# Second half of batch 0's heads by casting loads, and the opening of an attention and gated feed-forward kernel in another order

## The chip, the cores and the metric

The kernel runs on one core of one Trainium2 chip. The metric is the device time of one execution in microseconds (us); smaller is better. The kernel before was timed in five runs: 320.38 us in the median, from 320.23 to 320.91. A profile was taken of one further execution; its own time stands in the table below.

## What is computed

Eight batches of linear attention, whose normed result is the input of a gated feed-forward block with a residual:

```python
kv  = einsum('bhsd,bhse->bhde', k, v)          # b=8, h=8 heads, s=576 tokens, d=e=64
out = einsum('bhsd,bhde->bhse', q, kv)
x   = out / sqrt(mean(out*out, -1) + 1e-6) * g_norm      # reshaped to 4608 x 512
ffn = (gelu(x @ w_gate) * (x @ w_val)) @ w_out           # w_gate, w_val: 512 x 1536; w_out: 1536 x 512
y   = x + sigmoid(x @ w_res) * ffn
```

All inputs are float32 in memory; the kernel multiplies in float16 and accumulates in float32.

## The kernel before

**Blocks.** Of each batch's 576 tokens the first 512 make one block (4 tokens on each of 128 partitions); the last 64 of every batch are gathered in a ninth block at the end. The attention of the next batches is worked out beside the feed-forward of the present one, at places written out by hand. Every engine runs its instructions in the order in which the program records them; the schedule is manual. The engines are TensorE (PE in the profile), VectorE (DVE), ScalarE (ACT) and GpSimd (POOL). SyncE (SP) and POOL issue most of the transfers.

**The opening.** Batch 0 has nothing in front of it that could hide its attention, so it is done in pairs of heads (pr 0 to 3), in an order written out as a string of words, `opening` (L1294 to L1299). The words are run one by one by `f_piece` (L1243); a word is a name, the pair and, where it can be chosen, the engine (A = ACT, D = DVE, P = POOL). The words that the texts below use:

- `qc`, `kc`, `vc` (f_cast, L1134 and L1132): cast a pair of heads of q, k, v from float32 to float16.
- `qT` (L1158), `qo` (L1161): transpose q of a pair on PE into a PSUM bank, and copy it out.
- `kv` (L1169, L1175), `kvo` (L1178): the product of k and v of a pair, 4 matmuls for the 512 tokens and 2 for the last 64 (which `lk`, L1143, and `lv`, L1152, prepare), and its copy under a mask that keeps the two heads apart.
- `o` (L1184), `sq` (L1192), `rd` (L1195), `rt` (L1201), `ri` (L1205), `t` (L1209): q times kv, squares on ACT, their sums on DVE, root on ACT, reciprocal and scaling on DVE.
- `xT` (L1219), `xo` (L1226, L1224): transpose the result and copy it out times the norm's weight.
- `g`, `v` (L1235): the pair's part of the first two columns of `x @ w_gate` and `x @ w_val`, with weight columns 0 to 255 (`wg0`, `wv0`).
- `warm` (L1111): matmuls on zeros whose result is not used.
- `wg`, `wv` (L148): issue a load of weight columns on POOL; `wcg`, `wcv` (L1264): cast weight columns.

**Where the data come from.** A load issued on SP moves float32 as it is; one issued on POOL casts to float16 on its way. All of batch 0 comes through SP (L1039, L1055, L1077): heads 0 to 3 of q, of k, k's and v's last tokens, v; then pairs 2 and 3 of each; then weight columns 0 to 255 of both matrices. Casting is done by the engines: per pair one instruction each for q, k and v, and four for the weights. For batch 0 the casts of q and k also reorder from by-head to by-token (`[P, NJ, H, D]`), so that one pair's 128 columns of k are the stationary operand of one matmul. In later batches POOL's loads cast, k stays by head, and `kv_mm` (L208) uses 64 columns per matmul, one head each, in two halves of the PSUM partitions.

**What follows the opening.** From L410 on, PE runs the feed-forward of block 0 for weight columns 2 to 11, then L946, L430, L447 and the next block. POOL issues the loads of the other weights and of batch 1 (L148, L1600, L120 to L122, L109, L157); at most eight loads of POOL are under way, and the ninth waits for the first. PSUM has eight banks of 2 KB per partition: four taken in turn for the attention (`pattn`), four for the feed-forward (`pmoe`).

```python
    opening = """
    qc1P qc0A qT1 qT0 kc1P kc0A qo0D warm3 lk0D lv0P qo1A warm3 vc1D vc0A kv1 qc2A kv0 kvo1 kvo0 o1 kc2P qT2
    lk1P sq1 qo2D o0 warm3 warm2 vc2P sq0 lv1A rd1 kv2 qc3P rt1 kvo2 rd0 kc3A qT3 wg1 wv1 ri1 o2 rt0 t1 warm3 warm1 sq2 vc3D
    rd2 qo3A xT1 kv3 wg2 wcg0P rt2 kvo3 ri0 ri2 warm2 o3 t2 xo1A wcg1P sq3a wcv0P sq3b g1 xT2 rd3a wcv1P rd3b
    wv2 t0 rt3 xo2A wg3 wv3 v1 xT0 ri3 xo0A g2 v2 t3a t3b xT3a xT3b g0 xo3aA xo3bD gelu v0 g3a v3a g3b v3b
    """
```

Of the kernel before, what the change touches and what calls it, by code (L numbers as in the profile page):

```python
# [8 lines left out]
FP32 = mybir.dt.float32  # L9
FP16 = mybir.dt.float16  # L10
# [8 lines left out]
def kernel(  # L19
# [27 lines left out]
    WCS = (256, 256, 512, 512)  # L47
# [24 lines left out]
                self.turn.append(bank)  # L72
            return psum.tile(shape, dtype, tag=f"bank{bank}", name=name)

    pmoe, pattn = Banks(3, 1, 0, 2, opening=(0, 1, 2)), Banks(4, 5, 6, 7)

    def banks_behind():

# [14 lines left out]
    def rows4(t, b, lo, hi):  # L93
        return t[b, lo:hi, 0:M0, :].rearrange("h (p j) d -> p h (j d)", j=NJ)
# [55 lines left out]
    def load_wg(i):  # L150
        load_columns(wg_c, moe_w_gate, i)
# [38 lines left out]
    def halves(e):  # L190
        return slice(e * D, (e + 1) * D)
# [846 lines left out]
    def load_first(which, t, lo, hi):  # L1038
        nc.sync.dma_start(out=raw[0, which][:, lo:hi, :], in_=rows4(t, 0, lo, hi))  # L1039
# [22 lines left out]
    for which, t in (("q", q), ("k", k), ("v", v)):  # L1062
        load_first(which, t, 0, HH)
        if which == "k":
            load_first_last(0)
    for pr in range(NP // 2, NP):
        load_first("q", q, 2 * pr, 2 * pr + 2)
        load_first("k", k, 2 * pr, 2 * pr + 2)
        if pr == NP // 2:
            load_first_last(1)  # L1070
        load_first("v", v, 2 * pr, 2 * pr + 2)
    w_raw = {}
    for n, t in (("g", moe_w_gate), ("v", moe_w_val)):
        pool, tag = (stage, "qraw") if n == "g" else (qkvp, "k16")
        w_raw[n] = pool.tile([P, H, NJ * D], FP16, tag=tag, name=f"w{n}f")
        w_raw[n] = w_raw[n].rearrange("p a b -> p (a b)").bitcast(FP32).rearrange("p (c f) -> p c f", c=NP)
# [43 lines left out]
    first = {}  # L1120
# [4 lines left out]
    def of_pair(pr):  # L1125
        return slice(2 * pr, 2 * pr + 2), slice(pr * P, (pr + 1) * P)

    def f_cast(which, pr, copy):
        hs, _ = of_pair(pr)
        dst, src = b16_t[0, which], raw[0, which]  # L1130
        if which == "v":
            copy(out=dst[:, hs, :], in_=src[:, hs, :])  # L1132
        else:
            copy(  # L1134
                out=dst.rearrange("p j h d -> p h j d")[:, hs, :, :],
                in_=src.rearrange("p h (j d) -> p h j d", j=NJ)[:, hs, :, :],
            )

    def f_k_last(half, engs):

        raw_ = first_raw[0][half].rearrange("p (j d) -> p j d", j=2)
        for j, eng in enumerate(engs):
            eng.tensor_tensor(  # L1143
                out=first_last[0][:, j, half * HH : (half + 1) * HH, :],
                in0=raw_[:, j, None, :].to_broadcast([P, HH, D]),
                in1=of_head[:, :, None].to_broadcast([P, HH, D]),
                op=ALU.mult,
            )

    def f_v_last(half, copy):  # L1150
        raw_ = first_raw[1][half].rearrange("p (j d) -> p j d", j=2)
        copy(out=first_last[1][:, half], in_=raw_[:, :, None, :].to_broadcast([P, 2, 2, D]))  # L1152

    def f_qT(pr):
        q16 = b16_t[0, "q"].rearrange("p j h d -> p j (h d)")
        first["qT", pr] = ps = pattn.tile([P, NJ, P], FP16, tag="at", name="qtp")
        for j in range(NJ):
            nc.tensor.transpose(ps[:, j, :], q16[:, j, of_pair(pr)[1]], ident)  # L1158

    def f_qT_out(pr, copy):  # L1160
        copy(out=s0["qT"][:, :, pr, :], in_=first["qT", pr])  # L1161

    def f_kv(pr):

        first["kv", pr] = ps = pattn.tile([P, P], FP32, tag="at", name="kvp")
        k16 = b16_t[0, "k"].rearrange("p j h d -> p j (h d)")
        hs, cs = of_pair(pr)
        for j in range(NJ):
            nc.tensor.matmul(  # L1169
                ps, lhsT=k16[:, j, cs], rhs=b16_t[0, "v"][:, hs, j * D : (j + 1) * D], start=(j == 0), stop=False  # L1170
            )
        for j in range(2):
            kl = first_last[0][:, j].rearrange("p h d -> p (h d)")[:, cs]
            vl = first_last[1][:, pr // 2, j].rearrange("p e d -> p (e d)")
            nc.tensor.matmul(ps, lhsT=kl, rhs=vl, start=False, stop=(j == 1))  # L1175
# [2 lines left out]
        nc.vector.tensor_tensor(out=s0["kv2"][:, pr, :], in0=first["kv", pr], in1=mask, op=ALU.mult)  # L1178

    def f_o(pr):  # L1180
        pool, tag = (pmoe, "mm") if pr < 2 else (pattn, "at")
        first["o", pr] = ps = pool.tile([P, NJ, P], FP32, tag=tag, name="op")
# [31 lines left out]
        )  # L1214

    def f_xT(pr, j0, j1):
        first["xT", pr, j0] = ps = pattn.tile([P, j1 - j0, P], FP16, tag="at", name="xtp")
# [25 lines left out]
    def f_piece(word):  # L1243

        name = word.rstrip("0123abADP")
        rest = word[len(name) :]
        pr = int(rest[0])
        j0, j1 = {"a": (0, NJ // 2), "b": (NJ // 2, NJ)}.get(rest[1:2], (0, NJ))
        eng = rest[-1:]
        if name in ("qc", "kc", "vc"):  # L1250
            f_cast(name[0], pr, engines[eng])
        elif name == "lk":
            f_k_last(pr, (nc.gpsimd if eng == "P" else nc.vector, nc.vector))
        elif name == "lv":
            f_v_last(pr, engines[eng])
        elif name == "warm":
            keep_warm(pr)
        elif name == "wg":
            load_wg(pr)
        elif name == "wv":  # L1260
            load_wv(pr)
        elif name in ("wcg", "wcv"):
            cs = slice(2 * pr, 2 * pr + 2)
            engines[eng](out=(wg_c if name == "wcg" else wv_c)[0][:, cs, :], in_=w_raw[name[-1]][:, cs, :])  # L1264
# [22 lines left out]
    nc.vector.tensor_copy(out=g16, in_=gps)  # L1287

    keep_warm(3)

# [5 lines left out]
    lk1P sq1 qo2D o0 warm3 warm2 vc2P sq0 lv1A rd1 kv2 qc3P rt1 kvo2 rd0 kc3A qT3 wg1 wv1 ri1 o2 rt0 t1 warm3 warm1 sq2 vc3D  # L1296
    rd2 qo3A xT1 kv3 wg2 wcg0P rt2 kvo3 ri0 ri2 warm2 o3 t2 xo1A wcg1P sq3a wcv0P sq3b g1 xT2 rd3a wcv1P rd3b
    wv2 t0 rt3 xo2A wg3 wv3 v1 xT0 ri3 xo0A g2 v2 t3a t3b xT3a xT3b g0 xo3aA xo3bD gelu v0 g3a v3a g3b v3b
    """  # L1299

    def first_gval(ahead):
        hids[0] = hidp.tile([P, NF, NJ * P], FP16, tag="hid", name="hid")
        for word in opening.split():
            if word == "gelu":
# [33 lines left out]

    plans = [{} for _ in range(B + 1)]
    amid_out = {}  # L1340

    hold = consts.tile([1, 1], FP16, name="hold")

    def load_behind(b, x_of=None):

# [291 lines left out]
```

## Time and profile before

| what | value |
|---|---|
| median of 5 runs | 320.38 us |
| the profiled execution's own time | 320.35 us |
| its span, first to last instruction | 318.5 us |
| busy in the span: PE, DVE, ACT, POOL | 310.7, 274.8, 210.6, 186.8 us |
| granted TensorE clock, mean | 0.996 |
| first L410 matmul (the opening is over) | 20.70 us |
| transfers, 2 to 15 us | 333 to 374 GB/s in each whole microsecond from 3 on |
| transfers, 15 to 55 us | 192 to 222 GB/s |

How to read it: the profiled execution took 320.35 us, 1.85 us more than its span, and lies 0.03 us under the median, so lengths in its trace can be added to or taken from either number. Times in a timeline count from the span's start. In its lines, a start, a duration and a number of instructions (x4) stand for that many instructions run together; in brackets stands how long the engine sat idle before and what released it. A matmul's duration holds its way through the array, so of matmuls in a row the distance from start to start counts. In the chain of waits, which is followed back from the last instruction, the time belongs to whoever was late. The GB/s of a transfer count what lands: a casting load reads twice that, since a load of 262,144 float32 elements is listed with 512 KB.

### The profile page before, as it was taken

To read this page: it belongs to the slowest core of one execution; us is meant where nothing else is said; L and a number is where in the kernel's file an instruction comes from. 1 tells how busy PE (TensorE), PEld (TensorE's weight loads), DVE (VectorE), ACT (ScalarE), POOL (GpSimd) and SP (SyncE) were. 2 spreads that over 40 slices of the span, in tenths; PEclk is the share of its full clock that TensorE was granted. 3 is DMA by queue.
4 is the path that set the end of the run, shared out by engine and by line. 5 is a ranking of instruction groups with operands and counts; after the bars stand their busy time and mean duration, and the time that the engine had idled before them with its cause. 6 is when DMAs were issued, how large, how long until landed. Compare 5 with 4: busy or idle time off the path is not lost.

```text
span 318.5 us, 7756 instructions
## 1 busy us (share of the span) xinstructions
PE 310.7 (98%) x3044; PEld 247.0 (78%) x3044; DVE 274.8 (86%) x486; ACT 210.6 (66%) x385; POOL 186.8 (59%) x249
## 2 busy tenths in 40 slices
PE   8999999999999999999999999999999999999993
PEld 3544755444788888888888888888888888888882
DVE  5788889789898999989998999899988777897774
ACT  3773685465848794889487958795767467836760
POOL 2792351572869479756975687417751375396332
PEclk9999999999999999999999999999999999999998
DMA  7999999799994898569947995700340003001204
GB/s 250 330 203 205 194 206 192 174 156 178 171 112 93 189 156 80 98 201 143 92 82 217 126 108 84 215 5 0 69 148 2 0 3 135 0 2 49 85 2 132
DMA packets 76694, 38.90 MB, mean 122 GB/s; under 512 B 42098, under 2 KB 74354, under 8 KB 76658
## 3 DMA queue, kind: packets, MB, share of 16 engines
q0 software_dynamic: 38752, 17.17, 42.6%
q1 hardware_dynamic: 37328, 20.71, 25.8%
q8 instruction: 24, 0.39, 0.5%
q10 hardware_dynamic: 578, 0.52, 0.5%
q14 instruction: 12, 0.10, 0.1%
HBM read 38.80 MB, written 9.44 MB: 151 GB/s over the span
## 4 chain that ended last, share of the span: by engine, by line
PE 93%; DVE 2%; DMA 2%; SPq 1%; POOL 0%; issue 0%; DVEq 0%
PE Ag L946 12%; PE Av L946 12%; PE wA L515 12%; PE Fv L946 6%; PE Fg L946 6%; PE gps L410 5%; PE vps L410 5%; PE rA L566 4%; PE fps L447 3%; PE Ev L946 3%; PE Eg L946 3%; PE wF L515 3%; PE wE L515 3%; PE wD L515 3%; PE w L515 2%; PE rps L430 2%
## 5 line engine op out<-in xcount | busy, mean ns | idle before, releaser
L983 POOL TENSOR_TENSOR hid<-ge,c 128x512 f16<-128x512 f16 x22 | 25.5, 1161 | 38.4 <-ACT ge L977 38.4
L515 PEld LDWEIGHTS <-hid_s 128*128 128x128 f16 x384 | 37.6, 98 | 4.3
L946 PEld LDWEIGHTS <-wsv 128*128 128x128 f16 x352 | 34.1, 98 | 4.8 <-issue 0.7
L946 PEld LDWEIGHTS <-wsg 128*128 128x128 f16 x352 | 34.4, 98 | 4.0
L361 POOL TENSOR_TENSOR t<-t,g 128x512 f16<-128x512 f16 x32 | 37.1, 1188 | 0.0
L702 POOL TENSOR_TENSOR osb<-osb,t 128x512 f32<-128x512 f32 x28 | 34.1, 1245 | 0.0
L956 ACT COPY Eg<-Ag 128x512 f32<-128x512 f32 x22 | 12.8, 582 | 27.7 <-PE Ag L946 27.7
L515 PEld LDWEIGHTS <-hid 128*128 128x128 f16 x288 | 28.2, 98 | 3.5
L946 PEld LDWEIGHTS <-wg 128*128 128x128 f16 x264 | 25.8, 98 | 3.2
L946 PEld LDWEIGHTS <-wv 128*128 128x128 f16 x264 | 25.8, 98 | 3.0
L946 PE MATMUL Ag<-ts,wsg 128*128 128x256 f16 x176 | 26.4, 273 | 0.0
L946 PE MATMUL Av<-ts,wsv 128*128 128x256 f16 x176 | 26.4, 273 | 0.0
L967 DVE TENSOR_TENSOR Fg<-Ag,d 128x512 f32<-128x512 f32 x22 | 15.3, 697 | 11.3 <-ACT d L960 7.6
L258 DVE TENSOR_REDUCE ss<-sq 128x8 f32<-128x512 f32 x32 | 20.5, 679 | 1.7 <-ACT sq L253 1.7
L398 ACT ACTIVATE ge<-gps 128x512 f16<-128x512 f32 x20 | 11.7, 597 | 14.3 <-PE gps L410 14.1
L515 PE MATMUL wA<-wo_ts,hid_s 128*128 128x256 f16 x168 | 20.6, 273 | 0.0
L977 ACT ACTIVATE ge<-Eg 128x512 f16<-128x512 f32 x22 | 13.1, 597 | 10.3 <-PE Eg L946 10.3
L977 ACT ACTIVATE ge<-c 128x512 f16<-128x512 f32 x22 | 13.8, 625 | 7.7 <-DVE c L967 7.7
L345 DVE TENSOR_TENSOR t<-op,ny 128x512 f16<-128x512 f32 x28 | 18.4, 684 | 0.5 <-POOL ny L319 0.4
L967 DVE TENSOR_TENSOR c<-Ag,d 128x512 f32<-128x512 f32 x22 | 15.2, 689 | 4.1 <-PE Ag L946 4.1
L977 ACT ACTIVATE ge<-Fg 128x512 f16<-128x512 f32 x22 | 13.0, 591 | 8.4 <-PE Fg L946 6.3
L410 PE MATMUL gps<-xT,wg 128*128 128x512 f16 x72 | 18.5, 379 | 0.0
(219 smaller groups left out, 858.0 us busy)
## 6 DMA issues: line engine op xcount, KB each, us to landing
out_dram<-osb SPq DMA_DIRECT2D x14, 512.0 KB, 3.7
qraw<-in_q_dram POOLq DMA_DIRECT2D x7, 512.0 KB, 6.8
k<-in_k_dram POOLq DMA_DIRECT2D x7, 512.0 KB, 8.9
v<-in_v_dram POOLq DMA_DIRECT2D x7, 512.0 KB, 10.6
wg<-in_moe_w_gate_dram POOLq DMA_DIRECT2D x2, 512.0 KB, 8.6
wv<-in_moe_w_val_dram POOLq DMA_DIRECT2D x2, 512.0 KB, 9.2
wo<-in_moe_w_out_dram POOLq DMA_DIRECT2D x2, 512.0 KB, 13.6
out_dram<-osb SPq DMA_DIRECT2D x4, 256.0 KB, 4.5
```

Of the source, the lines that this page charges most:

```text
L258: nc.vector.tensor_reduce(out=out_, in_=sqs.pop((b, i)), op=ALU.add, axis=mybir.AxisListType.X)
L345: nc.vector.tensor_tensor(out=t, in0=o, in1=scale, op=ALU.mult)
L361: eng.tensor_tensor(out=t_t[blk][:, jj, :], in0=t_t[blk][:, jj, :], in1=g16, op=ALU.mult)
L410: nc.tensor.matmul(ps[:, j0 * P : j1 * P], lhsT=w[:, cc, :], rhs=xT_t[blk][:, j0:j1, cc, :], start=(cc == 0 and j0 == 0), stop=(cc == NP - ...
L515: nc.tensor.matmul(ps[:, e - es[0], :], lhsT=a[:, f, e * P : (e + 1) * P], rhs=b[:, f, :], start=(start and e == es[0] and f == 0), stop=( ...
L566: nc.tensor.matmul(out_[:, e, :], lhsT=x_[:, e, cc, :], rhs=w_[:, cc, :], start=(first and e == 0 and cc == 0), stop=(cc == 1), skip_group ...
L702: nc.gpsimd.tensor_tensor(out=res_all[of], in0=res_all[of], in1=t_t[blk][of], op=ALU.add)
L946: nc.tensor.matmul(out_[:, r, :], lhsT=lhsT, rhs=rhs, start=(first and r == 0 and c == 0), stop=(c == 1), skip_group_check=True,)
L956: nc.scalar.copy(out=tile_of("E", u), in_=ps["A", u])
L967: nc.vector.tensor_tensor(out=dst, in0=ps["A", u], in1=sb["d", u], op=ALU.add)
L977: nc.scalar.activation(out=ge[q], in_=source(q, "g"), func=AF.Gelu)
L983: eng.tensor_tensor(out=dst, in0=ge[q], in1=source(q, "v"), op=ALU.mult)
```

## The change

Three things are changed, all before 21 us.

1. SP loads only heads 0 to 3 of q, k and v, and all of the last 64 tokens. Heads 4 to 7 of q, k and v and weight columns 0 to 255 of `w_gate` come by casting loads on POOL, 256 KB each as they land, issued one after the other at the head of POOL's queue, behind a copy of one element (`hold`) that waits for the memset of a small tile on DVE. The load of the same columns of `w_val` is a word of the opening (`wv0`). The casts of pairs 2 and 3 and of the weights are gone.
2. Batch 0's q and k stay by head. So a pair's q is transposed by 8 instructions of 64 columns, not 4 of 128, and the 4 matmuls of `kv` for the 512 tokens become 8.
3. The words of the opening stand in another order, with 12 filler matmuls where there were 17, and the PSUM banks of the opening are named one by one (`BANK`).

```diff
-    pmoe, pattn = Banks(3, 1, 0, 2, opening=(0, 1, 2)), Banks(4, 5, 6, 7)
+    pmoe, pattn = Banks(3, 1, 0, 2, opening=(0,)), Banks(4, 5, 6, 7)
...
-        by_head = [P, H, NJ * D] if b > 0 else [P, NJ, H, D]
-        b16_t[b, "k"] = qkvp.tile(by_head, FP16, tag="k16", name="k16")
+        b16_t[b, "k"] = qkvp.tile([P, H, NJ * D], FP16, tag="k16", name="k16")
...
-    for pr in range(NP // 2, NP):
-        load_first("q", q, 2 * pr, 2 * pr + 2)
-        load_first("k", k, 2 * pr, 2 * pr + 2)
-        if pr == NP // 2:
-            load_first_last(1)
-        load_first("v", v, 2 * pr, 2 * pr + 2)
-    w_raw = {}
-    for n, t in (("g", moe_w_gate), ("v", moe_w_val)):
...
-        nc.sync.dma_start(out=w_raw[n], in_=t[:, 0 : WCS[0]].rearrange("(cc p) f -> p cc f", p=P))
+    load_first_last(1)
+    hold = consts.tile([1, 1], FP16, name="hold")
...
     for t in last_kv[0] + last_kv[1]:
         nc.vector.memset(t[R:P], 0.0)
+    nc.gpsimd.tensor_copy(out=hold, in_=last_kv[0][0][R : R + 1, 0, 0:1])
+    q0 = b16_t[0, "q"].rearrange("p j h d -> p (j h d)").rearrange("p (h x) -> p h x", h=H)
+    for dst, t in ((q0, q), (b16_t[0, "k"], k), (b16_t[0, "v"], v)):
+        nc.gpsimd.dma_start(out=dst[:, HH:H, :], in_=rows4(t, 0, HH, H))
+    load_wg(0)
...
+    BANK = {"qT": (7, 6, 6, 7), "kv": (5, 4, 4, 5), "o": (2, 1, 6, 7), "xT": (5, 4, 4, 6), "xTb": (0, 0, 0, 5)}
+
     def f_qT(pr):
...
         for j in range(NJ):
-            nc.tensor.transpose(ps[:, j, :], q16[:, j, of_pair(pr)[1]], ident)
+            for e in range(2):
+                nc.tensor.transpose(ps[halves(e), j, :], q0[:, 2 * pr + e, j * D : (j + 1) * D], ident)
...
         for j in range(NJ):
-            nc.tensor.matmul(
-                ps, lhsT=k16[:, j, cs], rhs=b16_t[0, "v"][:, hs, j * D : (j + 1) * D], start=(j == 0), stop=False
-            )
+            ds = slice(j * D, (j + 1) * D)
+            for e in range(2):
+                nc.tensor.matmul(
+                    ps[halves(e), :],
+                    lhsT=b16_t[0, "k"][:, 2 * pr + e, ds],
+                    rhs=b16_t[0, "v"][:, hs, ds],
+                    start=(j == 0),
+                    stop=False,
+                )
...
-            f_k_last(pr, (nc.gpsimd if eng == "P" else nc.vector, nc.vector))
+            f_k_last(pr, (nc.gpsimd, nc.gpsimd if eng == "P" else nc.vector))
...
     opening = """
-    qc1P qc0A qT1 qT0 kc1P kc0A qo0D warm3 lk0D lv0P qo1A warm3 vc1D vc0A kv1 qc2A kv0 kvo1 kvo0 o1 kc2P qT2
...
+    qc1D qc0A qT1 qT0 g16 warm3 kc1D kc0A lk0D lv0P wv0 wg1 qo1D qo0A warm2 vc1D vc0A kv1 kv0 kvo1 lk1P kvo0 lv1A o1 o0
+    qT2 qT3 sq1 sq0 wv1 wg2 rd1 rd0 qo2A rt1 ri1 qo3A rt0 t1 warm2 warm2 wv2 wg3 wv3 kv2 kvo2 kv3 kvo3 ri0 t0 xT1 o2 o3
+    sq2 xo1A rd2 sq3 rt2 warm3 g1 rd3 xT0 xo0A ri2 v1 t2 rt3 g0 ri3 xT2 xo2A v0 t3a t3b xT3a xT3b g2 xo3aA xo3bD gelu
+    v2 g3a v3a g3b v3b
     """
+    pattn.turn = [5, 4, 6, 7]
```

More of the change, by code (lines that the diff above doesn't have):

```diff
@@ L1065 @@
             load_first_last(0)
-    for pr in range(NP // 2, NP):
-        load_first("q", q, 2 * pr, 2 * pr + 2)
-        load_first("k", k, 2 * pr, 2 * pr + 2)
-        if pr == NP // 2:
-            load_first_last(1)
-        load_first("v", v, 2 * pr, 2 * pr + 2)
-    w_raw = {}
-    for n, t in (("g", moe_w_gate), ("v", moe_w_val)):
-        pool, tag = (stage, "qraw") if n == "g" else (qkvp, "k16")
-        w_raw[n] = pool.tile([P, H, NJ * D], FP16, tag=tag, name=f"w{n}f")
-        w_raw[n] = w_raw[n].rearrange("p a b -> p (a b)").bitcast(FP32).rearrange("p (c f) -> p c f", c=NP)
-        nc.sync.dma_start(out=w_raw[n], in_=t[:, 0 : WCS[0]].rearrange("(cc p) f -> p cc f", p=P))
+    load_first_last(1)
+    hold = consts.tile([1, 1], FP16, name="hold")
     ident32 = moep.tile([P, P], FP32, tag="ge", name="ident32")
@@ L1129, in f_cast @@
         hs, _ = of_pair(pr)
[L1130 to L1136, printed above, removed]
-            )
+        dst, src = q0 if which == "q" else b16_t[0, which], raw[0, which]
+        copy(out=dst[:, hs, :], in_=src[:, hs, :])
     def f_k_last(half, engs):
@@ L1152, in f_v_last @@
         copy(out=first_last[1][:, half], in_=raw_[:, :, None, :].to_broadcast([P, 2, 2, D]))
+    BANK = {"qT": (7, 6, 6, 7), "kv": (5, 4, 4, 5), "o": (2, 1, 6, 7), "xT": (5, 4, 4, 6), "xTb": (0, 0, 0, 5)}
     def f_qT(pr):
-        q16 = b16_t[0, "q"].rearrange("p j h d -> p j (h d)")
-        first["qT", pr] = ps = pattn.tile([P, NJ, P], FP16, tag="at", name="qtp")
+        first["qT", pr] = ps = pattn.tile([P, NJ, P], FP16, name="qtp", bank=BANK["qT"][pr])
         for j in range(NJ):
-            nc.tensor.transpose(ps[:, j, :], q16[:, j, of_pair(pr)[1]], ident)
+            for e in range(2):
+                nc.tensor.transpose(ps[halves(e), j, :], q0[:, 2 * pr + e, j * D : (j + 1) * D], ident)
     def f_qT_out(pr, copy):
@@ L1163, in f_kv @@
     def f_kv(pr):
-        first["kv", pr] = ps = pattn.tile([P, P], FP32, tag="at", name="kvp")
-        k16 = b16_t[0, "k"].rearrange("p j h d -> p j (h d)")
+        first["kv", pr] = ps = pattn.tile([P, P], FP32, name="kvp", bank=BANK["kv"][pr])
         hs, cs = of_pair(pr)
         for j in range(NJ):
-            nc.tensor.matmul(
-                ps, lhsT=k16[:, j, cs], rhs=b16_t[0, "v"][:, hs, j * D : (j + 1) * D], start=(j == 0), stop=False
-            )
+            ds = slice(j * D, (j + 1) * D)
[7 more added lines that the diff above has]
+                )
         for j in range(2):
@@ L1180, in f_o @@
     def f_o(pr):
-        pool, tag = (pmoe, "mm") if pr < 2 else (pattn, "at")
-        first["o", pr] = ps = pool.tile([P, NJ, P], FP32, tag=tag, name="op")
+        first["o", pr] = ps = pattn.tile([P, NJ, P], FP32, name="op", bank=BANK["o"][pr])
         for j in range(NJ):
@@ L1216, in f_xT @@
     def f_xT(pr, j0, j1):
-        first["xT", pr, j0] = ps = pattn.tile([P, j1 - j0, P], FP16, tag="at", name="xtp")
+        bank = BANK["xTb" if j0 else "xT"][pr]
+        first["xT", pr, j0] = ps = pattn.tile([P, j1 - j0, P], FP16, name="xtp", bank=bank)
         for j in range(j0, j1):
@@ L1261, in f_piece @@
             load_wv(pr)
-        elif name in ("wcg", "wcv"):
-            cs = slice(2 * pr, 2 * pr + 2)
-            engines[eng](out=(wg_c if name == "wcg" else wv_c)[0][:, cs, :], in_=w_raw[name[-1]][:, cs, :])
         elif name == "qo":
@@ L1286 @@
     nc.tensor.matmul(gps, lhsT=ones16, rhs=grow16.rearrange("p h d -> p (h d)"), start=True, stop=True)
-    nc.vector.tensor_copy(out=g16, in_=gps)
     keep_warm(3)
     opening = """
-    qc1P qc0A qT1 qT0 kc1P kc0A qo0D warm3 lk0D lv0P qo1A warm3 vc1D vc0A kv1 qc2A kv0 kvo1 kvo0 o1 kc2P qT2
-    lk1P sq1 qo2D o0 warm3 warm2 vc2P sq0 lv1A rd1 kv2 qc3P rt1 kvo2 rd0 kc3A qT3 wg1 wv1 ri1 o2 rt0 t1 warm3 warm1 sq2 vc3D
-    rd2 qo3A xT1 kv3 wg2 wcg0P rt2 kvo3 ri0 ri2 warm2 o3 t2 xo1A wcg1P sq3a wcv0P sq3b g1 xT2 rd3a wcv1P rd3b
-    wv2 t0 rt3 xo2A wg3 wv3 v1 xT0 ri3 xo0A g2 v2 t3a t3b xT3a xT3b g0 xo3aA xo3bD gelu v0 g3a v3a g3b v3b
+    qc1D qc0A qT1 qT0 g16 warm3 kc1D kc0A lk0D lv0P wv0 wg1 qo1D qo0A warm2 vc1D vc0A kv1 kv0 kvo1 lk1P kvo0 lv1A o1 o0
+    qT2 qT3 sq1 sq0 wv1 wg2 rd1 rd0 qo2A rt1 ri1 qo3A rt0 t1 warm2 warm2 wv2 wg3 wv3 kv2 kvo2 kv3 kvo3 ri0 t0 xT1 o2 o3
+    sq2 xo1A rd2 sq3 rt2 warm3 g1 rd3 xT0 xo0A ri2 v1 t2 rt3 g0 ri3 xT2 xo2A v0 t3a t3b xT3a xT3b g2 xo3aA xo3bD gelu
+    v2 g3a v3a g3b v3b
     """
+    pattn.turn = [5, 4, 6, 7]
     def first_gval(ahead):
@@ L1303, in first_gval @@
         for word in opening.split():
-            if word == "gelu":
+            if word == "g16":
+                nc.vector.tensor_copy(out=g16, in_=gps)
+            elif word == "gelu":
                 nc.scalar.preload_act_table_set("gelu_and_others")
@@ L1340 @@
     amid_out = {}
-    hold = consts.tile([1, 1], FP16, name="hold")
     def load_behind(b, x_of=None):
```

## The prediction

> **What bounds the kernel now.** I read the waits of PE first. From 20 us to the end that view lists no wait at all: once the opening is over, PE runs through, 298 us of it. So a change before 21 us is worth the shift of one moment, the first L410 matmul, as long as nothing behind it comes late. Call that moment S. It is 20.70 us:
>
> ```profile
> 20.48 0.38 PE L1235 MATMUL vps<-xT,wv 128*128 128x256 f16 x2
> 20.70 1.03 PE L410 MATMUL gps<-xT,wg 128*128 128x512 f16 x4
> ```
>
> The chain of waits tells how S comes about. Up to 10 us it is a transfer on SP's queue, then POOL's casts, then DVE's small steps, and only the last 3 us are PE:
>
> ```profile
> 4.31 5.30 DMA kf<-in_k_dram
> ...
> 10.24 0.78 POOL kf L1143
> ```
>
> The timeline gives the steps of DVE, which I use as price list: cast of v on landing, two masked copies, sums, scaling.
>
> ```profile
> 8.11 0.43 DVE L1132 CAST v<-hid_s 128x512 f16<-128x512 f32 x1 [0.28 <-DMA hid_s<-in_v_dram]
> 9.32 0.63 DVE L1178 TENSOR_TENSOR t<-kvp,mask 128x128 f16<-128x128 f32 x2 [0.79 <-PE kvp L1175]
> ...
> 12.37 0.68 DVE L1195 TENSOR_REDUCE ss<-sq 128x8 f32<-128x512 f32 x1
> ...
> 13.19 0.69 DVE L1209 TENSOR_TENSOR t<-op,rinv 128x512 f16<-128x512 f32 x1
> ...
> 14.80 0.29 DVE L1178 TENSOR_TENSOR t<-kvp,mask 128x128 f16<-128x128 f32 x1
> ```
>
> Start to start, a sum takes 0.59, a scaling 0.61. The last masked copy (pair 3) starts at 14.80, 5.90 before S.
>
> **What goes.** Six casts and four weight casts (0.43 to 0.65 each) leave DVE, ACT and POOL. In the changed order the queue of DVE is: cast v, two copies, two sums, reciprocal, scaling of pair 1, and then the copies of pairs 2 and 3. So S hangs on two landings: L, of v's heads 0 to 3 on SP (8.08 before, 0.03 ahead of the cast), and T, of v's heads 4 to 7 on POOL.
>
> **Landing T, the rates.** SP's loads move 333 to 374 GB/s. POOL's land 196 to 212 from 15 us on, so they read about 400. The stretches (the last two columns are the share of the DMA engines and GB/s):
>
> ```profile
> 14.00:15.00 1.00, 1.00 (x12) 0.74 (x13) 1.00 (x3) 0.50 (x2) 1.00 (x2) 1.00 1.10 341
> 15.00:16.00 1.00, 0.76 (x7) 0.36 (x5) 0.96 (x4) 1.00 (x4) 0.82 (x2) 1.00 1.41 212
> 16.00:17.00 1.00, 0.80 (x7) 0.36 (x6) 1.00 (x4) 0.46 (x3) 0.88 (x2) 1.00 1.45 196
> ```
>
> **When POOL's data start.** The memset that `hold` waits for ends at 3.12; a `hold` takes 0.18 and leaves a gap of 0.32 before the next issue (110.05 to 110.55). First issue: 3.65. From issue to first packet it takes 1.7 us where SP is quiet (110.55 to 112.2), but 2.65 where SP's loads fill the engines:
>
> ```profile
> 12.16 0.98 POOL L148 DMA_DIRECT2D wg<-in_moe_w_gate_dram  x1
> ```
>
> Its queue q0 has its first 12 packets only in the half microsecond from 14.5:
>
> ```profile
> q1 hardware_dynamic: 162, 0.16, 101.8%
> q0 software_dynamic: 12, 0.01, 8.9%
> ```
>
> Bounds 5.35 and 6.3. SP's queue is full here, so I take 6.3.
>
> **The price of sharing.** Where both queues have work (71.5 to 72 us, SP stores), they split the engines evenly:
>
> ```profile
> q0 software_dynamic: 84, 0.04, 60.9%
> q1 hardware_dynamic: 50, 0.10, 59.9%
> ```
>
> Before 6.3 SP has moved 1.43 MB (the sums by microsecond); v's last byte is its 1.70th MB. The first 0.3 us of the sharing cost SP little (104% and 77% beside POOL's first packets), 0.09 MB; the other 0.19 MB at half of 350 GB/s take 1.08. Last byte 7.68, and 0.98 later it counts as landed (before: 7.1, released 8.08): **L = 8.65**, 0.57 later than now. Bounds: 8.1 (no disturbance) and 9.3 (start at 5.35, half rate at once but for POOL's slow first microsecond).
>
> POOL gets some 100 GB/s until SP is done at 8.4 (0.18 MB), and 200 then. Its 3 x 262 KB end at 11.45, land 0.98 later, at 12.4. In the lone loads at 110 us the third one lands later than such a sum by about a microsecond (10.1 us after issue); these are half the size. I take 0.2: **T = 12.6**, bounds 12.0 and 13.4.
>
> The Trainium skill, page "DMA: Bandwidth & Descriptors", section "Rules for kernel authors", says spreading loads over several issuing engines gains no bandwidth, since the same 16 engines move them; the rows above differ, because a casting load reads more per microsecond. With 347 GB/s of reading for POOL too, 1.57 MB would take 4.5 in place of 3.9, and S by it would be 0.6 later.
>
> The page "SBUF — State Buffer", section "SBUF: two separate sides", warns that DVE's casts from float32 can lock GpSimd out while it writes a load's descriptors. The three issues from 12.16 took 0.98, 0.78 and 0.77 with DVE 99% busy, so no stretch is seen; by the page DVE's casts between 4.66 and 6.5 (two casts and `g16`, 1.5 us) could put T at 14 and S at 22.
>
> **64 columns instead of 128.** No row shows this shape with 128 moving columns. From below: nothing, since L208 runs 40 matmuls of 64 columns in 0.75 us, 19 ns each, the two heads side by side. From above: eight one behind the other are 4 x 55 ns more, 0.22, and the change of width costs 0.11 (after such a group the next four matmuls take 0.97 instead of 0.86), perhaps twice: 0.44.
>
> ```profile
> 41.69 0.75 PE kvp L208 x40
> 42.44 0.97 PE fps L447 x4
> ```
>
> I take 0.2 per `kv`. It counts twice on the path from L (kv1, and kv0 ahead of the second copy) and twice from T. The transposes of q have slack.
>
> **The sum.** From L: cast 0.43 to 9.11; kv1 0.70 (0.50 now) to 9.84; copy and `o1` to 10.60; square 0.58, first sum from 11.24, second to 12.5; ACT has the square of pair 0 and `qo2` ahead of the root, so the root ends 12.58; reciprocal, scaling: DVE is free for pair 2's copy at 13.47. From T: kv2 to 13.35, kv3 to 13.89. So the copy of pair 3 starts at 13.92, 0.88 earlier than now. But behind it stands more: the scaling of pair 0 (to 15.05), the sums of pairs 2 and 3, the second from 16.10 because ACT squares pair 3 only behind pair 2's square and a copy `xo1` (14.36 + 0.55 + 0.58 + 0.58), reciprocal, scaling of pair 2 (to 17.55), reciprocal, scaling of pair 3 in halves to 18.55, transposes and `xo3b`. PE starts `g2` at 18.79 when `xo2` is out, then `v2` (0.43 each) and four steps of 0.22: **S = 20.53**. That is L + 11.88 and T + 7.93, both; against 20.70 the break-even is L = 8.82 or T = 12.77. What DVE was freed of comes back as waiting for T and ACT. The change is worth 0.17 us: 320.35 - 0.17 = **320.2**, 0.06% under the median.
>
> **Cover.** Weights for `g1` (15.61) and `v1` (16.26) land at T + 1.3 and T + 2.6, slack 1.7 and 1.1; if they are later, the in-order PE holds `xT0` and `g0` too. Columns 512 on of `w_val` are the tightest now (landed 24.63, first used 25.02); in the new queue they land near 23.5. Everything behind keeps its order at most 1.7 earlier, and each load waits for the eighth before it as now. New waits: `hold` has all loads behind it; POOL's two `lk1` wait for k's last tokens (about 9.4) with `wv1` behind them, which has 10 us. A fifth of a per cent, 0.64 us, is about what a measurement can tell.
>
> **Rivals.**
> - *SP is not disturbed and the heads run side by side* (faster). POOL's packets come when SP is nearly done: L = 8.1, T = 12.0, nothing for 64 columns. L + 11.5 = 19.6: 319.25; with 0.1 for the columns and L = 8.4, 20.0: 319.65. For it: POOL's late first packets at 14.8. Against: the even split. Chance 0.33.
> - *SP's v starves behind POOL's loads* (slower). The place is v's last 0.6 MB on SP from 5.35 on; each us that L passes 8.82 costs one, and from L = 9.46 on it shows. L = 9.6, T = 13.0: 21.48, 321.1. For it: an even split from the first packet. Against: the slow starts at 112 us. Chance 0.25, in which I count a related loss: fillers run at 0.43 us each until 8.6 and 0.21 later; with 12 instead of 17 the array could fall back, and matmuls of the opening would take double.
> - *It doesn't do what it says*: the second half lands no earlier than its casts end now (14.2) because the same bytes come through the same engines. That is T = 14, S = 21.9, 321.6; it counts to slower.
>
> **The numbers.** No difference within 0.2% 0.42, faster 0.33, slower 0.25. The likeliest case alone: 319.8 to 320.9. The range must reach into both others: 319.2 (the best L and T) to 321.8 (T = 14, or 9.3 and 0.3 for the columns with something on top).
>
> **What would show it.** S in the timeline against 20.53; the cast of v (L) at 8.7; kv2 at 12.65 released by a transfer; DVE without a gap from 9.9 to 18.6 but before the last sums; the sums by microsecond still over 330 GB/s until 6.3. I am wrong if PE waits for weights after S, if the array's steps stay doubled after 9 us, or if T comes before 12.

## The result, and the profile after

The changed kernel takes 321.56 us in the median of 43 runs (320.06 to 323.52), the kernel before 320.62 in 80 (320.20 to 322.98): a ratio of 1.0024, interval 1.0015 to 1.0033, so slower by 0.8 us (the two medians alone differ by 0.94). I had forecast 320.2 and no difference as the likeliest. The profiled execution took 321.92 us with a span of 320.1; before, 320.35 and 318.5.

From 22.3 us on, the waits of PE list nothing, as before from 20 on. So the loss in this execution is the shift of S, the first matmul behind the opening, which went from 20.70 to 22.32: 1.62 us, all of the 1.6 by which the span grew. It is more than the 0.8 of all runs, so this execution is one of the slower ones. The timeline of the changed kernel (start, duration, engine, line, tiles; in brackets the idle time and what ended it):

```profile
5.53 0.77 POOL L1097 DMA_DIRECT2D v<-in_v_dram  x1
...
8.22 0.43 DVE L1125 CAST v<-hid_s 128x512 f16<-128x512 f32 x1 [0.86 <-DMA hid_s<-in_v_dram]
...
14.38 0.41 PE L1160 MATMUL kvp<-v,k 128*64 128x128 f16 x8 [1.12 <-DMA v<-in_v_dram]
...
15.62 0.29 DVE L1173 TENSOR_TENSOR t<-kvp,mask 128x128 f16<-128x128 f32 x1 [0.27 <-PE kvp L1170]
...
22.32 1.03 PE L409 MATMUL gps<-xT,wg 128*128 128x512 f16 x4
```

Read it from the landings. L, the cast of v's heads 0 to 3, is at 8.22: SP's loads were hardly disturbed (8.11 before; I had said 8.65). T is late: POOL issues v's heads 4 to 7 at 5.53, and PE starts pair 2's kv only at 14.38, released by that transfer, where I had 12.65. The copy of pair 3 is at 15.62 in place of 14.80. The chain of waits says the same in one line:

```profile
5.53 8.72 DMA v<-in_v_dram
14.25 0.14 issue
```

From its issue on, the transfer is 8.72 us under way and nothing else is on the path: T = 14.25 against the forecast 12.6. From kv2 (the start of pair 2's kv) to S it is 7.94 us, where the prediction had 7.88 (20.53 - 12.65); from T to S it is 8.07, where it had 7.93. So the way from T to S was right within 0.14, and T's size was wrong.

### The profile page after: what moved, and what is told of

Read it like the earlier page. It is cut to its first block, busy times and chain, and to the rows that moved or that the text cites. A ratio compares the mean times of both kernels' runs of the same rounds, so it can differ in the third digit from the quotient of the medians.

```text
span 320.1 us, 7794 instructions
## 1 busy us (share of the span) xinstructions
PE 311.5 (97%) x3071; PEld 246.7 (77%) x3071; DVE 274.2 (86%) x483; ACT 209.8 (66%) x383; POOL 187.4 (59%) x248
## 4 chain that ended last, share of the span: by engine, by line
PE 93%; DMA 3%; DVE 1%; issue 1%; POOL 1%; ACT 1%; DVEq 0%; POOLq 0%
PE Ag L945 12%; PE Av L945 12%; PE wA L514 11%; PE Fv L945 6%; PE Fg L945 6%; PE gps L409 5%; PE vps L409 5%; PE rA L565 4%; PE fps L446 3%; PE Eg L945 3%; PE Ev L945 3%; PE wE L514 3%; PE wF L514 3%; PE wD L514 3%; DMA v<-in_v_dram 3%; PE w L514 2%
## 5 line engine op out<-in xcount | busy, mean ns | idle before, releaser
L955 ACT COPY Eg<-Ag 128x512 f32<-128x512 f32 x22 | 12.8, 582 | 27.7 <-PE Ag L945 27.7
L397 ACT ACTIVATE ge<-gps 128x512 f16<-128x512 f32 x20 | 11.8, 597 | 14.4 <-PE gps L409 14.2
L976 ACT ACTIVATE ge<-Eg 128x512 f16<-128x512 f32 x22 | 13.1, 597 | 10.3 <-PE Eg L945 10.3
L409 PE MATMUL vps<-xT,wv 128*128 128x512 f16 x72 | 18.5, 379 | 0.0
## 6 DMA issues: line engine op xcount, KB each, us to landing
wg<-in_moe_w_gate_dram POOLq DMA_DIRECT2D x2, 512.0 KB, 13.4
```

The costliest lines, as they stand in the source:

```text
L409: nc.tensor.matmul(ps[:, j0 * P : j1 * P], lhsT=w[:, cc, :], rhs=xT_t[blk][:, j0:j1, cc, :], start=(cc == 0 and j0 == 0), stop=(cc == NP - ...
L955: nc.scalar.copy(out=tile_of("E", u), in_=ps["A", u])
L976: nc.scalar.activation(out=ge[q], in_=source(q, "g"), func=AF.Gelu)
```

## The experiments

Each run is compared with the kernel before on the same chip; in the changed kernel kv2 is released by the landing of POOL's third load.

**The changed kernel twice more** (labels a_again and a_third). It tells how far a single trace can be trusted.

> The changed kernel once more, for a second profile. In the first one S (first matmul of L409) is 22.32 us, the second half of v lands at 14.25 and DVE ends the scaling t1 at 14.31. If both moments are set by the program, S comes out at 22.3 within 0.2 again and the time near 321.6. If the array's step from slow to full rate (first matmul group with 0.22 us per four 128-column matmuls: 10.6 us here, 8.8 us in the kernel before) wanders from run to run, that moment differs by a microsecond or more, and S with it by some tenths.

> The changed kernel once more, beside the next three on one chip. Both theories: ratio 1.0015 to 1.0035, kv2 between 13.8 and 14.6 in the profiled execution. Theory A (a slow ramp of POOL's queue makes T late): the DMA share from 8 to 12 us below 1.40 where T is late. Theory B (chance of the single execution): kv2 may as well come at 13.

Measured: 1.0025 (1.0008 to 1.0042) and, on another chip, 1.0059 (1.0040 to 1.0078). kv2 at 14.06 and 13.26, S at 21.99 and 21.18. The same program with the same issues thus lands its third load over a microsecond earlier or later. In a_third's trace:

```profile
13.26 0.41 PE L1160 MATMUL kvp<-v,k 128*64 128x128 f16 x8 [1.09 <-DMA v<-in_v_dram]
...
21.18 1.03 PE L409 MATMUL gps<-xT,wg 128*128 128x512 f16 x4
```

Again 7.92 from kv2 to S. Behind S this execution loses more: S is 0.48 later than in the kernel before, the span 1.2 (319.7). At 80 us PE waits once, and its weight load names an SP transfer of a later batch's q:

```profile
80.55 0.52 PEld L229 LDWEIGHTS <-qT 64*128 64x128 f16 x32 [1.17 <-DMA qT<-q]
80.55 0.64 PE L229 MATMUL op<-kv,qT 64*128 64x64 f16 x32 [0.68 <-ACT th L438]
```

Such a wait of 0.7 to 0.8 us stands in the traces of e3, e4, d1, d3 and n1 as well, one of 0.33 in b1, and none in the others, after and a_again among them. So a difference in time between two executions is not always one of S, and what follows is read from kv2 and S.

Over the nine runs in which kv2 waits for POOL's third load:

| run | kv2 | S | S - kv2 |
|---|---|---|---|
| after | 14.38 | 22.32 | 7.94 |
| a_again | 14.06 | 21.99 | 7.93 |
| a_third | 13.26 | 21.18 | 7.92 |
| e1_v_last_later | 14.34 | 22.27 | 7.93 |
| e6_weights_later | 13.94 | 21.87 | 7.93 |
| d1_hold_longer | 13.06 | 20.99 | 7.93 |
| d2_hold_longer_again | 13.37 | 21.30 | 7.93 |
| n1_sp_without_q | 13.42 | 21.35 | 7.93 |
| d3_hold_14 | 16.16 | 24.09 | 7.93 |

Whatever else differs in them, S follows kv2 one for one.

**What else is late: ACT, and the landing taken away** (e1, e2, e3). ACT's copy of v's last tokens stood ahead of the squares and waited for a small load of SP:

```profile
11.19 0.41 ACT L1140 CAST hid_s<-th 128x256 f16<-128x256 f32 x1 [2.35 <-DMA th<-in_v_dram]
```

e1 puts it behind them, e2 leaves out POOL's load of q's heads 4 to 7 (pairs 2 and 3 use q of pairs 0 and 1), so that v is POOL's second load, and e3 does both.

```diff
-... kvo0 lv1A o1 o0 qT2 qT3 sq1 sq0 wv1 ...       (e1, e3)
+... kvo0 o1 o0 qT2 qT3 sq1 sq0 lv1A wv1 ...
...
-    for dst, t in ((q0, q), (b16_t[0, "k"], k), (b16_t[0, "v"], v)):     (e2, e3)
+    for dst, t in ((b16_t[0, "k"], k), (b16_t[0, "v"], v)):
```

> The copy of v's last tokens (lv1) stands behind the two squares on ACT, so the squares no longer wait for the small load that lands at 11.19. Theory 'first half' (the chain from v's first half to t1 sets S): the squares start 0.45 earlier, S falls from 22.3 to 21.9 and the time by 0.45 to about 321.1. Theory 'landing' (the second half of v on POOL, at 14.25, sets S): t1 ends 0.45 earlier, but kv2 still starts at 14.38; S stays at 22.3, time 321.6. If both are equally late, also no change.

> Leaves out the load of q's heads 4 to 7 on POOL (the transposes of pairs 2 and 3 read heads 0 to 3 in their place), so k and v come one load of 256 KB earlier. Theory 'landing': v's second half lands 1.3 us earlier, near 12.9, and S falls by about that, to 21.0, time 320.3. Theory 'first half': v lands earlier all the same, but t1 ends at 14.3 and S stays at 22.2 to 22.3, time 321.5. Both equally late: the same as 'first half', with kv2 starting at 13 and DVE's copy of pair 2 at 14.3.

> Both edits at once (leaves out the load of q's heads 4 to 7, and the copy of v's last tokens stands behind the squares). Theory 'landing': as without the second edit, S 21.0. Theory 'first half': as with the second edit alone, S 21.9. Both equally late: more than either alone, S 21.5 to 21.8 and the time near 320.9, limited by t1 at 13.9.

| run | ratio (interval) | kv2 | S |
|---|---|---|---|
| e1 | 1.0025 (1.0009 to 1.0040) | 14.34 | 22.27 |
| e2 | 1.0010 (0.9997 to 1.0024) | 12.99 | 21.22 |
| e3 | 0.9995 (0.9982 to 1.0009) | 12.45 | 20.77 |

ACT's wait alone is worth nothing (e1). With a load fewer ahead of v, S falls by 1.1, and then the first half is what is late: pair 1's scaling on DVE at 13.38 in e2, whose chain of waits has the small load that ACT waits for, and not POOL's:

```profile
4.35 6.59 DMA th<-in_v_dram
...
13.38 0.69 DVE t L1203
```

Only then does ACT's wait count, 0.45 from e2 to e3. So a second path stood close behind T: in the changed kernel DVE sits idle for 0.75 us ahead of pair 2's copy, in a_again for 0.59, in a_third for 0.21.

**The issues earlier** (e4). POOL's `hold` is dropped; the first issue goes from 3.81 to 1.43.

```diff
-    nc.gpsimd.tensor_copy(out=hold, in_=last_kv[0][0][R : R + 1, 0, 0:1])
```

> The changed kernel without the copy of `hold`, so that POOL's loads are issued as early as POOL gets to them, some 2.4 us sooner; same bytes, same work. Theory A (the landing T of v's heads 4 to 7 sets S, and it is late because POOL's first packets come 3.3 us after the issue and its queue then ramps up slowly): T comes 1.5 to 2.4 sooner, the first matmul of pair 2's kv at 12 to 12.7 in place of 14.38; S then falls to what the first half allows, 21.2 to 21.6, less if SP is not disturbed at all. Theory B (the 16 DMA engines are simply full, so the total sets T): T stays within 0.5 of 14.25 and what POOL starts sooner SP loses: L, the cast of v's heads 0 to 3, goes from 8.2 to over 9.2, and S stays at 22.0 to 22.4 or rises. The ratio to before: 1.000 to 1.002 by A, 1.002 to 1.004 by B.

Measured: 1.0158 (1.0129 to 1.0188), S at 25.40. A miss for both theories in size, though theory B had the direction, and the rival that I had called "SP's v starves" in full: SP's v lands at 12.36.

```profile
12.39 0.43 DVE L1124 CAST v<-hid_s 128x512 f16<-128x512 f32 x1 [3.47 <-DMA hid_s<-in_v_dram]
```

The queues in e4 from 6 to 7 us (packets, MB, and the time that they took as a share of 16 engines; q0 is POOL's, q1 SP's):

```profile
q0 software_dynamic: 248, 0.13, 95.3%
q1 hardware_dynamic: 134, 0.06, 32.6%
```

Alone, SP moves 0.36 MB in a microsecond (4 to 5 us). Beside POOL's casting loads it is left 0.05 to 0.10 in each from 5 to 9, and 0.17 to 0.18 from 9 to 11: the sharing is not even at first, and SP loses most. `hold` is what keeps the first half alive.

**The issues later** (d1, d2, d3): the copy of `hold` 4, again 4, and 14 times, in place of once.

> The changed kernel with the copy of `hold` four times in place of once, so that POOL issues its loads some 0.55 us later (first issue 4.35 in place of 3.81). It tells why POOL's first packets came at 7.0. Theory A (they wait until the backlog of SP's loads is worked off, whenever they were issued): first packets again at 7.0 to 7.3, L at 8.1 to 8.3, pair 2's kv at 14.1 to 14.5, S 22.0 to 22.4, ratio 1.002 to 1.003. Theory B (a fixed delay of 3.2 us from issue to first packet): first packets at 7.5 to 7.7, kv2 and S 0.4 to 0.6 later: S 22.6 to 22.9, ratio 1.004.

> The copy of `hold` four times, as before (first issue 4.11). Theory A (a little later issue avoids the overlap with SP's tail, so that all 16 engines come to POOL's loads at the same time): kv2 again at 12.9 to 13.5, S 20.9 to 21.5, ratio to before 0.8 to 1.6 us under the changed kernel's in this call, 1.000 to 1.001. Theory B (chance): kv2 anywhere from 13 to 14.4, ratio as the changed kernel's within 0.3 us.

> The copy of `hold` fourteen times: POOL's first issue at about 5.1, 1.3 us later than in the changed kernel. Theory A: POOL's packets start at 7.5 to 8.3, behind SP's bulk, at the full rate at once; 0.786 MB at 200 GB/s and 1 us to landing: kv2 at 13.0 to 13.8, so no later than in the changed kernel in spite of the later issue; the copy of v's last tokens on ACT not later than 10; S 20.9 to 21.7, ratio 1.000 to 1.0015. Theory B (T hangs on the issue): kv2 1.0 to 1.4 later than in the changed kernel, 15.2 to 15.7, S 23.1 to 23.6, ratio 1.005 to 1.007.

d1 and d2 issue at 4.11: ratios 1.0004 (0.9983 to 1.0026) and 1.0047 (1.0029 to 1.0065), kv2 at 13.06 and 13.37. That is sooner than in after, a_again and e1, but d2's is not sooner than a_third's (13.26), which ran on the same chip. The intervals of d2 and a_third (1.0059) overlap too, so neither a gain nor a loss from issuing 0.3 us later is shown. d3 missed its aim: 14 copies delay the first issue to 6.84 (not 5.1), and POOL's copy of v's last tokens of heads 0 to 3, queued behind the issues, held PE for 2.4 us. 1.0140 (1.0127 to 1.0154); kv2 at 16.16. What it shows: with SP quiet, POOL's first packets come 1.8 us after the issue (8.6), and the third load lands 7.2 us after its own, where the changed kernel needs 7.6 to 8.7.

**SP done sooner, and the weights later** (n1, e6). n1 leaves out SP's load of q (q of pairs 0 and 1 is cast from zeros); e6 issues `wg0`, `wv0`, `wg1` behind `lk1P`.

```diff
-    for which, t in (("q", q), ("k", k), ("v", v)):     (n1)
+    for which, t in (("k", k), ("v", v)):
...
-    load_wg(0)                                           (e6)
-... lk0D lv0P wv0 wg1 qo1D ... kvo1 lk1P kvo0 ...
+... lk0D lv0P qo1D ... kvo1 lk1P wg0 wv0 wg1 kvo0 ...
```

> The changed kernel without SP's load of q's heads 0 to 3 (left out: q of pairs 0 and 1 is cast from a tile of zeros), so that SP has 1.05 MB to move in place of 1.57 and is done some 1.4 us sooner; POOL's issues stay where they are. Theory A (POOL's data wait for SP's backlog): first packets at 5.6 to 6.2, v's second half 1.0 to 1.5 sooner, kv2 at 12.9 to 13.4, S 20.9 to 21.4, ratio 0.999 to 1.001. Theory B (fixed delay from issue): first packets at 7.0 as before, only the sharing with SP's tail goes; kv2 at 13.6 to 14.2, S 21.5 to 22.1, ratio 1.001 to 1.003.

> The changed kernel with the first weight columns issued only behind the masking of k's last tokens on POOL (about 10.5 in place of 6.3), so that nothing stands behind q, k and v in POOL's queue while they move. Theory A (v's bytes are through at 12.2, and it lands only at 14.25 because the 16 engines are uneven and those that are ahead already work on the weights): kv2 0.5 to 1.0 sooner, 13.4 to 13.9; S is then set by the weights, which come 1 to 2 us later, so it is to be read from kv2 and not from S or the time. Theory B (the weights behind take nothing from v): kv2 at 14.1 to 14.5 as in the changed kernel, S 22.5 to 24 by the weights. Ratio 1.001 to 1.008 by either.

n1: 1.0016 (0.9996 to 1.0035), kv2 13.42. It doesn't decide: SP's v came only some 0.5 sooner (7.64) and SP's queue was at work until past 7 all the same; POOL's first 5 packets are in the half microsecond from 6.5, most from 7. e6: 1.0023 (0.9999 to 1.0047), kv2 13.94, inside the spread of the unchanged program. Neither a backlog of SP nor the weights behind v is shown to be the cause.

**Another order of the three loads** (e5): k, v, q in place of q, k, v, with q's transposes behind pair 3's kv, and e1's edit. Same bytes, same instructions.

```diff
-    for dst, t in ((q0, q), (b16_t[0, "k"], k), (b16_t[0, "v"], v)):
+    for dst, t in ((b16_t[0, "k"], k), (b16_t[0, "v"], v), (q0, q)):
```

> The changed kernel with POOL's three loads in the order k, v, q in place of q, k, v, the transposes of q's pairs 2 and 3 (and their copies) behind the masked copy of pair 3, and the copy of v's last tokens behind the squares. The same bytes and the same instructions. Theory A (what counts is when v's second half lands, not how much is moved): v lands 1 to 1.5 sooner, pair 2's kv starts at 12.7 to 13.3, and what is late next is q, at 14.2, so that o2 starts at 15.0 to 15.5; S 21.3 to 21.8, ratio 1.000 to 1.002. Theory B (the whole amount on the engines sets the end): S unchanged, 22.0 to 22.4, ratio 1.002 to 1.003.

Measured: 1.0009 (0.9994 to 1.0025), kv2 at 12.10, S at 21.10. v's landing is off the path, as theory A had it, and what is late next is q, now the third load: it lands at 13.24, its transposes start at 13.31, and S is 7.86 behind the landing. In the changed kernel S is 8.07 behind the landing of the third load, so by these lengths the order is worth 0.2. But in this trace q is not alone on the path. The cast of v's heads 0 to 3 came only at 8.77 (8.22 in the changed kernel), and the chain of waits goes through that landing and PE's own order up to the transposes:

```profile
3.13 5.62 DMA hid_s<-in_v_dram
...
13.07 0.22 PE kvp L1170 x2
13.29 0.02 issue
13.31 0.43 PE qtp L1148 x8
```

So q's landing and the first half came level here. That the third load came a microsecond sooner lies inside the spread of a_again and a_third; whether the order did it, this run can't say.

**v's second half back on SP** (h1), as float32 and cast by POOL.

```diff
+    load_first("v", v, HH, H)
-    for dst, t in ((q0, q), (b16_t[0, "k"], k), (b16_t[0, "v"], v)):
+    for dst, t in ((b16_t[0, "k"], k), (q0, q)):
-... sq1 sq0 wv1 ...
+... sq1 sq0 vc2P vc3P lv1A wv1 ...
```

> A half-way version: v's heads 4 to 7 go back to SP as float32, behind heads 0 to 3, and are cast by POOL; POOL loads k and q (heads 4 to 7) and the first weight columns, in the order k, q; the copy of v's last tokens stands behind the squares. Theory A (POOL's queue is late, SP's is not): v's second half is there at about 10, POOL's casts of it end by 11.8, k lands at 12.0 to 12.7, pair 2's kv starts at 12.2 to 12.8 and S is set by the first half or by q's landing at 12.8 to 13.5: 20.6 to 21.4, ratio 0.9985 to 1.0015. Theory B (total bytes): 1.5 of them are now float32 for SP too, k lands no earlier than v did, at 14, and S stays at 22.

A miss: 1.0083 (1.0055 to 1.0111), S at 23.75. SP's queue stays full to 8.5, POOL's first packets come only shortly before (from 8.2, 4.4 us after the issue at 3.82), and q lands at 12.77. The in-order PE has q's transposes ahead of all of pair 2:

```profile
12.82 0.75 PE L1149 MATMUL qtp<-ident,q 128*64 128x128 f16 x16 [1.54 <-DMA q<-in_q_dram]
```

I had left that order as it was. The fillers behind them took 0.43 each, twice the 0.21 of other runs there.

**The 64-column form** (b1, w1). b1 is the kernel before with part 2 of the change alone; w1 is e5 with heads 0 to 3 by token and pairs 0 and 1 in 128 columns again.

```diff
-            nc.tensor.matmul(ps, lhsT=k16[:, j, cs], ...)                     (b1; q's transposes alike)
+            for e in range(2):
+                nc.tensor.matmul(ps[halves(e), :], lhsT=b16_t[0, "k"][:, 2 * pr + e, ds], ...)
...
+            if pr < 2:                                                         (w1, on e5)
+                nc.tensor.matmul(ps, lhsT=by_tok(b16_t[0, "k"])..., rhs=b16_t[0, "v"][:, hs, ds], ...)
+                continue
```

> The kernel before with one part of the change alone: batch 0's q and k stay by head, so that the transposes of q are 8 of 64 columns and each kv has 8 matmuls of 64 columns in place of 4 of 128. Order and loads are those of before. If the narrow form is the dear part of the change (rival), two kv on the path from L cost 0.4 or more and the half-rate array doubles it: S from 20.70 to 21.1 to 21.5, ratio 1.001 to 1.003. If it is cheap (my theory, 0.2 per kv, and the last masked copy at 14.80 has POOL's casts before it, not PE): S 20.6 to 20.9, ratio 0.999 to 1.001.

> POOL's order k, v, q as in the run of that order, and batch 0's heads 0 to 3 by token again, so that q's transposes and the kv matmuls of pairs 0 and 1 have 128 columns; pairs 2 and 3 stay by head. All the work is done. My theory (0.2 us for each narrow kv on the path, and the first half is what is late next when v lands sooner): the masked copies of pairs 1 and 0 come 0.14 and 0.3 sooner than in the run without this edit, counted from the cast of v; S 20.7 to 21.0 in place of 21.10, ratio 0.999 to 1.001. Rival (the narrow form is free here, its cost in the kernel before came from the order there): S within 0.1 of 21.10, ratio 1.0009 again. If the narrow form costs what the median of the run by head alone says (1.1 us), the ratio falls to 0.998.

b1: 1.0036 (1.0021 to 1.0051). I had expected no shift of S; it is 21.13, 0.43 later. The masked copy that before stood at 14.80:

```profile
15.23 0.29 DVE L1178 TENSOR_TENSOR t<-kvp,mask 128x128 f16<-128x128 f32 x1 [0.22 <-PE kvp L1175]
```

Two kv in series on DVE's path, 0.14 to 0.22 each (kv2 to its copy 0.67, before 0.53; from one kv to the next behind it 0.56, before 0.34): the size of the term was right, that it has cover in the old order was wrong. The wait at 80 us adds 0.33 here. The profiled execution of b1 is its fastest of 12 (321.12, median 322.35), 0.77 over that of the kernel before, so the rest of its 1.1 us is not in this trace and stays open. w1: 1.0011 (0.9988 to 1.0035), S at 20.09, but its profiled execution (319.84) too is its fastest, median 321.33. Counted from the cast of v, the copies of pairs 1 and 0 come at 1.08 and 1.4 in place of 1.25 and 1.81 in e5: the wide form is cheaper by about what I expected. S is set by the third load again, q at 12.26, 7.83 before it; in w1 and in c1 below the chain of waits goes through its transfer (first w1, then c1):

```profile
5.55 6.71 DMA q<-in_q_dram
```

```profile
5.94 6.94 DMA q<-in_q_dram
```

So whether the third load carries v or q, S can hang on it.

**All that paid, together** (c1): w1 with `hold` four times.

> All the work, with the three edits that paid: POOL's order k, v, q with q's transposes behind pair 3's kv and the copy of v's last tokens behind the squares; heads 0 to 3 by token with 128 columns; `hold` four times. If the terms add (theory A), v's second half is never what is late, S is set by the first half and by ACT's copies at 20.1 to 20.6, and the ratio to before is 0.9975 to 0.9995. If it is chance that made S 20.1 in the run without the longer hold (theory B), ratio 1.0005 to 1.0015 as there.

Measured: 1.0002 (0.9993 to 1.0011), 320.39 to 320.99 in 11 runs, S at 20.70, exactly that of the kernel before, 7.82 behind the third load (12.88). All eleven runs lie under the fastest of a_third on the same chip (321.22), so together the edits win back what the change had lost; which of them does how much isn't shown. It doesn't beat the kernel before, and no run that does all the work has a median under that of the kernel before on its chip. In this trace POOL's queue comes up evenly. First the changed kernel, then c1, by microsecond (the last two columns are the share of the DMA engines and GB/s):

```profile
8.00:9.00 1.00, 1.00 (x3) 0.15 (x1) 0.43 (x1) 0.62 (x1) 1.00 (x3) 1.00 1.29 172
9.00:10.00 1.00, 1.00 (x13) 0.62 (x14) 0.00 (x0) 0.00 (x0) 0.99 (x2) 1.00 1.32 176
10.00:11.00 1.00, 1.00 (x14) 0.76 (x15) 0.42 (x2) 0.00 (x0) 1.00 (x3) 1.00 1.34 176
11.00:12.00 1.00, 0.78 (x17) 0.55 (x17) 0.16 (x1) 0.81 (x3) 1.00 (x2) 1.00 1.36 183
```

```profile
9.00:10.00 1.00, 0.95 (x16) 0.76 (x14) 0.58 (x2) 0.03 (x1) 1.00 (x2) 1.00 1.43 193
10.00:11.00 1.00, 1.00 (x8) 0.40 (x6) 0.40 (x1) 1.00 (x3) 1.00 (x3) 1.00 1.45 196
```

c1 is near the full share from 9 on (1.43, then 1.45); the changed kernel only from 12 on (1.46). c1's third load lands 6.94 us after its issue at 5.94, at 12.88, and 1.1 after its last packet by count; the changed kernel's at 14.25, 2.2 after.

## Why the prediction was wrong, step by step

- **The failed step** is the size of one term: "POOL gets some 100 GB/s until SP is done at 8.4 (0.18 MB), and 200 then. Its 3 x 262 KB end at 11.45, land 0.98 later, at 12.4 ... I take 0.2: T = 12.6, bounds 12.0 and 13.4". To 8.4 it held: first packets at 7.0 rather than 6.3, but faster, 0.17 MB. Then POOL moved some 168 GB/s and not 200 (the rest of the 0.79 MB up to 12.05, by the count of packets): 0.60 lost. And the landing came 2.2 behind the last packet by that count in place of 1.15: 1.05 lost. Together 1.65; S is 1.79 over the forecast 20.53.
- **The bounds.** 13.4 was the far end for T; the four executions with the changed kernel's issues and order of loads gave 13.1, 13.9, 14.2 and 14.25. I had a single row for a third load behind two others (the lone one, a microsecond later than the sum) and took 0.2 of it for being half the size. In this execution the full microsecond was nearer; in a_again (13.92, packets through at 12.07) the lag was 1.85, and in a_third (13.12 and 11.97) 1.15, as I had said. So the slower rate, 0.5 to 0.6, is in all three traces of the changed kernel, and the late landing behind it is in two.
- **S = T + 7.93** was right within 0.14 (8.07 here), and the part from kv2 on, 7.88 by my sum, was 7.92 to 7.94 in nine runs. **L + 11.88** was not: the scaling of pair 1 came at 13.62 where my sum had 12.8, because the array was still at half rate for the first kv (0.64 for 8 matmuls, 0.41 later) and ACT waited for v's last tokens. Steps that stay doubled after 9 us I had named as a sign of being wrong, and they did, until 10.5. Neither cost anything here: e1 takes ACT's wait away, a_again has the full rate from 8.77 on, and S stays at 22.27 and 21.99. But this second miss lay hidden under the first: in e2, where v's second half is in time, S is still 21.22, 0.7 over the forecast.
- **L = 8.65**: 8.22, better than forecast. POOL's packets came when SP was nearly done, as in my first rival. But that rival had T at 12.0, and here T came late all the same, by what happened behind 8.4.
- **SP's v starves**: not in the changed kernel, thanks to `hold`, but e4 shows the price when it goes: 5 us against the kernel before. I had put the sharing at an even split; SP gets less.
- **It doesn't do what it says** (T = 14, S = 21.9, 321.6, for the reason that the same bytes come through the same engines): by its numbers it is what came, 14.25 and 321.56, but not for that reason: in w1 and c1 three loads of the same size are in at 12.26 and 12.88. The far end of my forecast (321.8) was put there for this rival, so that 321.56 still lies inside it is luck: the reason given for it isn't borne out.
- **The narrow form**, 0.2 per kv: right in size (0.14 to 0.22 in b1).
- **Nothing late behind S**: true of the first trace, but not of all executions (the wait at 80 us in a_third).
- **DVE's locking of POOL's descriptors**, which the page "SBUF — State Buffer" of the Trainium skill warns of in "SBUF: two separate sides": POOL's four issues took 0.98 and then 0.77 to 0.78, as they did where DVE was full; no stretch is seen there. Its T of 14 came out all the same, but no view here shows that it was by this way.

What stays open: why POOL's queue needs until 12 us to reach its full share in some executions and only until 9 in others. It goes with the program in these traces, so it is hardly chance alone: a share of 1.43 or more comes from 9 on in d1, d2, e5, w1 and c1 (a longer `hold`, or k and v ahead of q), and only from 10 to 12 on in the changed kernel's three traces, e1, e6 and n1 (q first, a single `hold`). No run shows why. That single engines are behind is my guess, since by the count of packets the three loads are through at 12.05 and the third isn't in before 14.25; it wasn't seen. The Trainium skill, page "DMA: Bandwidth & Descriptors", section "Latency and other measured facts", says that two of the 16 engines are usually slower, with a guess that ring traffic of POOL's own descriptors slows them; it would fit, but no view here separates the engines. The same page, section "Queues, rings and completion order", has each engine take turns between queues by packets; e4's packets (248 and 134 from 6 to 7 us, 172 and 168 from 9 to 10) differ from an even split at first and agree with it later.

## What to carry to other kernels

A load that is third in a queue need not land where the sum of its bytes ends: here it came 0.7 (w1) to 2.2 us behind that, by the count of packets. Price it by the spread of landings in rows of the same kind, which here was 13.12 to 14.25 in one program and 12.26 to 14.25 over two orders of the loads, at the same issue times. Casting loads that start while plain loads of another queue still run can take half and more from them (e4), so a small wait ahead of them can be worth more than the earlier start. And where one path becomes late by a landing that varies between executions, one trace shows one draw of it: profile the kernel again before taking its size.

## What the runs showed of the hardware that I had not expected

- From POOL's issue to its first packet: 1.8 us with SP quiet (d3), 3.0 to 3.2 in the changed kernel, d1 and c1, 3.6 in e4 (5.0), 4.4 behind a longer SP queue (h1). Neither a fixed delay nor the end of SP's queue fits all five.
- A 64 KB load that SP issued at 4.35 let its reader start only at 11.19, 6.8 us later, behind POOL's casting loads; in d1 it was there at 9.86.
- The array's step from half to full rate wandered between executions of the same program, from 8.8 us at the latest (a_again) to 10.5 (after), after fillers and small matmuls that had begun at 1.2 (with short gaps), while the granted clock read 1.00. The Trainium skill, page "TensorE: Matmul & The Clock Gate", section "Part 1: The HAM clock gate (the "warmup" mystery)", has the full rate after about 3.4 us of sustained work; here it came 7.6 to 9.3 us after the first filler.
